# Fused attention and two feed-forward layers: a half tile moved as a half, and two norm rows passed through DRAM

## The chip, the cores and the metric

One core of a Trainium2 chip runs the whole program. The metric is the device time of one execution in microseconds. Matmuls run on TensorE (PE in the rows, its weight loads PEld), elementwise work on VectorE (DVE) and ScalarE (ACT), a few things on GpSimd (POOL); SyncE (SP) issues most transfers, GpSimd the rest.

## What is computed

Four batches of sigmoid attention (12 heads, 448 rows, head size 64) give x of 1792 rows and 768 columns. Then:

```
rms = sqrt(mean(x * x, axis=-1) + 1e-6);  xn = x / rms * rms_g
g = xn @ w_gate;  val = xn @ w_val            # 768 -> 1536
x = (g * sigmoid(g) * val) @ w_out            # 1536 -> 768
h = x @ w_in2                                 # 768 -> 2048
out = (h - tanh(h)) @ w_out2                  # 2048 -> 768
```

All tensors are float32.

## The kernel before

Data lies transposed: channels on the 128 partitions, the 448 rows of a batch along the free axis. A product of two float32 matrices is three matmuls of rounded high parts and low remainders (high by high, high by low, low by high; lines 919 to 923 and 976 to 981), each of 128 x 128 weights on 448 columns.

The two layers work on pairs of batches, (0, 1) and then (2, 3). Two 2 x 2 blocks of weights and of activations are multiplied with seven block products instead of eight (names A11 to S4 on the left, B11 to T4 on the right; lines 819 and 820). Phases Ag and Av are the products with w_gate and w_val, B the one with w_out, C with w_in2, D with w_out2. A job is one pair of weight rows of a phase Ag, Av or C (`seven_units`, 21 groups of three matmuls), or a set of four in B and D (`set_units`; `plain_units`, without the seven-product scheme, for some sets). Jobs for batches (0, 1) come before those for (2, 3) within a layer.

**The left factors.** In its first use, a pair's raw weights are loaded (`load_raw`, 768 KB each), unpacked (`values32`), summed into factors (`sums`, lines 491 to 498) and split into high and low parts (`factors`). `keep` (line 508) also stores the factors in DRAM, in four pieces: (A11, A12), (S1, S2), (S3, S4) and A22. For the pairs that are not in `SPLIT` each piece is a whole tile of 128 x 768 numbers, 384 KB, stored by `put` from SyncE (line 470): 6 pairs of w_gate, 6 of w_val and 6 of w_in2. The tile of the fourth piece holds A21 and A22 as alternating blocks of 128 columns, and only A22 is used later (`one_of`, line 401). In the second use, for batches (2, 3), `two` (line 553) loads each piece with `again` (line 519, 384 KB) and splits it.

**The norm.** In attention `x_end` adds up the squares of x by batch. `norm` (line 671) sums them over the partitions with four one-column matmuls into a bank of PSUM (line 677), scales (line 681, VectorE) and raises to the power -0.5 (line 683, GpSimd): a tile `rc` of 112 x 4 numbers, one for each of the 448 rows. `clear_norm` writes zeros to the bank with one matmul. `spread_norm` (line 691) brings these numbers to all 128 partitions: four VectorE multiplications with an identity matrix (line 698), one float32 matmul with ones (line 702) and a ScalarE copy (line 706). `x_whole` (line 767, its instruction line 770, VectorE) multiplies x with them. For batches 2 and 3 x is put in DRAM (line 669) and reloaded (line 713).

**Order.** All work is entered with `add` into a plan, in program order, with a cost in ns per engine, what it reads and writes, and `after`, the ns until its result is there (`LAND` 4500 and `FAR` 10000 for transfers). `Plan.issue` then simulates the engines: of the work that can start soonest on its engine it takes the one whose deadline is earliest, and writes the instructions out in that order. So every engine runs a fixed order, SyncE too, whose transfers wait in line behind an instruction that waits. A change of a cost or of the program order can change the order on every engine. `mixed` (line 1097) and the list `beside` (line 1129) say beside which units of the main work other work is entered. The norms of batches 2 and 3 are entered beside the last attention batch and behind it (lines 1120 to 1122); their spreads, with `x_units`, from the last job of phase Av of batches (0, 1) to the first job of phase Ag of batches (2, 3) (line 1130). Sums of phases B and D are accumulated in DRAM by GpSimd's transfers with an addition (line 795).

Of the kernel before, what the change touches and what calls it, by code (L numbers as in the profile page):

```python
# [21 lines left out]
P = 128  # L22
# [237 lines left out]
def tile_sigmoid_attention_moe_moe(  # L260
# [38 lines left out]
    def bank(kind="mm"):  # L299
        return slot(kind, ps_p, [P, 512], F32, "ps")  # L300

    def unit(kind, dt=F32):
        return slot(kind, unit_p, [P, S], dt, "unit")
# [85 lines left out]
    def values32(r):  # L389
# [8 lines left out]
            op0=ALU.logical_shift_right, op1=ALU.bitwise_or), [r["t"], z["t"]], [c[0], c[1]])  # L398
        return c

    def one_of(t, x):

        return t.rearrange("p (k e c) -> p e k c", e=2, c=P)[:, x]
# [5 lines left out]
    def factors(j, names, of, reads):  # L409


        n = len(names)
        t = slot("op", wt_p, [P, 2, n, NH], F32R, "wt")
        w = lambda q: t.tile[:, q].rearrange("p n h -> p (n h)")
        hi, lo = (lambda: w(0), lambda: w(1)) if n == 2 else (
            lambda q=q: w(q).rearrange("p (k c) -> p k c", c=P) for q in range(2))
        split(n * NH, hi, lo, of, reads, [t["h"]], [t["l"]])
        use_factors(j, names, t)
        return t
# [62 lines left out]
    def pair_units(ph, i, rs, j):  # L482
        c = []
        d = stored[ph, i] = Slot(None, lambda: dram_p.tile([P, 4, 2, NW], F32, name=f"w{ph}_{i}") if (ph, i) in SPLIT else
                                 dram_p.tile([P, 4, NW], F32, name=f"w{ph}_{i}"))

        def total(to, n, x, y, sub=True):
            add({**dve(NH, psum=False), **pool(NH)}, lambda e: (ENG[e].tensor_sub if sub else ENG[e].tensor_add)(
                one_of(to.tile, n), one_of(x[0].tile, x[1]), one_of(y[0].tile, y[1])), [x[0][x[1]], y[0][y[1]]], [to[n]])

        def sums():
            t = slot("cv", cv_p, [P, NW], F32, "cv")
            a11, a12, a21, a22 = ((x, n) for x in c for n in range(2))
            total(t, 0, a21, a22, sub=False)
            total(t, 1, (t, 0), a11)
            total(c[0], 0, a11, a21)
            total(c[0], 1, a12, (t, 1))
            c.append(t)

        def two(n, names, at):  # L500
            x = c[n]
            keep(None if j is None else factors(j, names, lambda: x.tile, [x[0], x[1]]), at, x)

        def last():
            x = c[1]
            keep(None if j is None else factors(j, ["A22"], lambda: one_of(x.tile, 1), [x[1]]), 3, x)

        def keep(t, at, x):
            if (ph, i) not in SPLIT:
                put(d, at, x)  # L510
                return
            add({"SP": (2200, False)}, lambda e: nc.sync.dma_start(
                out=d.tile[:, at, :, :t.tile.shape[2] * NH], in_=t.tile.bitcast(F32).rearrange("p q n h -> p q (n h)")),
                [t["h"], t["l"]], [d[at]], after=LAND)

        return [lambda: c.append(values32(rs[0])), lambda: c.append(values32(rs[1])), lambda: two(0, ("A11", "A12"), 0),
                sums, lambda: two(2, ("S1", "S2"), 1), lambda: two(0, ("S3", "S4"), 2), last]

    def again(d, at):
        w = slot("again", cv_p, [P, NW], F32, "cv")  # L520
        add({"SP": (1100, False)}, lambda e: nc.sync.dma_start(out=w.tile, in_=d.tile[:, at]), [d[at]], [w[0], w[1]], after=LAND)
        return w
# [18 lines left out]
    def again_units(j):  # L541
        ph, _, i, _ = jobs[j]
        if (ph, i) in SPLIT:
            d = stored[ph, i]

            def load_parts(at, names):
                t = slot("op", wt_p, [P, 2, len(names), NH], F32R, "wt")
                add({"SP": (2200, False)}, lambda e: nc.sync.dma_start(
                    out=t.tile.bitcast(F32).rearrange("p q n h -> p q (n h)"), in_=d.tile[:, at, :, :len(names) * NH]), [d[at]], [t["h"], t["l"]], after=LAND)
                use_factors(j, names, t)  # L550

            return [lambda at=at, names=names: load_parts(at, names) for at, names in enumerate(FACTORS)]
        def two(at, names):
            t = again(stored[ph, i], at)
            of = lambda: t.tile
            if len(names) == 1:
                factors(j, names, lambda: one_of(of(), 1), [t[1]])
            else:
                factors(j, names, of, [t[0], t[1]])

        return [lambda at=at, names=names: two(at, names) for at, names in enumerate(FACTORS)]

# [108 lines left out]
    def norm(b):  # L671
        sq = sqs.pop(b)
        ps = bank("nm")
        ms, rc = (Slot(None, lambda t=t: norm_p.tile([TK, 4], F32, tag=t, name=t)) for t in ("ms", "rc"))
        def sums(e):
            for i in range(4):
                nc.tensor.matmul(  # L677
                    ps.tile[:TK, i:i + 1], lhsT=sq.tile[:, i * TK:(i + 1) * TK], rhs=ones[:, 0:1], start=True, stop=True)

        add({"PE": (1500, False)}, sums, [sq["t"]], [ps["t"]], stream="norm")  # L680
        add(dve(4), lambda e: nc.vector.tensor_scalar(
            out=ms.tile, in0=ps.tile[:TK, :4], scalar1=1.0 / DM, scalar2=EPS, op0=ALU.mult, op1=ALU.add), [ps["t"]], [ms["t"]])
        add({"POOL": (950, True)}, lambda e: nc.gpsimd.tensor_tensor(out=rc.tile, in0=ms.tile, in1=expo, op=ALU.pow),
            [ms["t"]], [rc["t"]])
        rcs[b] = rc, ps

    def clear_norm(b):
        ps = rcs[b][1]
        add({"PE": (250, False)}, lambda e: whole_bank(ps.tile), [], [ps["t"]], stream="norm")

    def spread_norm(b):
        (rc, _), ps2 = rcs.pop(b), bank("nm")
        dg = unit("sq")
        r = rstd[b] = unit("rstd")

        def spread(e):
            for i in range(4):
                nc.vector.tensor_scalar(
                    out=dg.tile[:TK, i * TK:(i + 1) * TK], in0=id_sb, scalar1=rc.tile[:, i:i + 1], scalar2=None, op0=ALU.mult)

        def rows(e):
            nc.tensor.matmul(ps2.tile[:, :S], lhsT=ones[:TK, :], rhs=dg.tile[:TK, :], start=True, stop=True)  # L702

        add({"DVE": (760, True)}, spread, [rc["t"]], [dg["t"]])
        add({"PE": (1500, False)}, rows, [dg["t"]], [ps2["t"]], stream="norm")
        add(act(S, psum=True), lambda e: nc.scalar.copy(r.tile, ps2.tile[:, :S]), [ps2["t"]], [r["t"]])
# [344 lines left out]
    def attn_units(b):  # L1051
        units = []
        for at in range(b * HP, (b + 1) * HP, 2):
            for x in (at, at + 1):
                units.append(lambda x=x: pair_qk(*pairs[x], (0, 1)))
                units.append(lambda x=x: (get_ready(x + 3), pair_qk(*pairs[x], (2, 3))))
            for x in (at, at + 1):
                units.append(lambda x=x: (pair_av(*pairs[x]), pair_end(*pairs[x])))
        return units
# [29 lines left out]
    def by_dve(units):  # L1089
        def run(u):  # L1090
            plan.copies_by = "DVE"
            u()
            plan.copies_by = None

        return [lambda u=u: run(u) for u in units]

    def mixed(units, *others):


        at = [0] * len(others)  # L1100
        for u in units[:2]:
            u()
        units = units[2:]
        for n, u in enumerate(units):
            u()
            for k, o in enumerate(others):
                while at[k] < (n + 1) * len(o) // len(units):
                    plan.later = BESIDE
                    o[at[k]]()
                    plan.later = 0  # L1110
                    at[k] += 1
# [5 lines left out]
    mixed(attn_units(2), [lambda: norm(1), lambda: clear_norm(1), lambda: spread_norm(1), *x_units("A", BATCHES[0], False)], rows_b[at[1]:at[2]])  # L1117
    for j in range(AHEAD):
        load(j)
    mixed(attn_units(3), [lambda: norm(2), lambda: clear_norm(2)], [u for j in range(AHEAD) for u in (*by_dve(conv(j)), lambda j=j: load(j + AHEAD))], rows_b[at[2]:])  # L1120
    norm(3)
    clear_norm(3)
    gates.clear()


# [1 line left out]
    first = {(ph, bs): [j for j in range(len(jobs)) if jobs[j][0] == ph and jobs[j][1] == bs][0] for ph in ("Ag", "C") for bs in BATCHES}  # L1127
    last = {(ph, bs): [j for j in range(len(jobs)) if jobs[j][0] == ph and jobs[j][1] == bs][-1] for ph in ("Av", "C") for bs in BATCHES}
    beside = [
        (last["Av", BATCHES[0]], first["Ag", BATCHES[1]], [lambda: [spread_norm(b) for b in BATCHES[1]], *x_units("A", BATCHES[1], True)], BEHIND),  # L1130
        (last["Av", BATCHES[1]], first["C", BATCHES[0]], x_units("C", BATCHES[0], True), BEHIND),
        (last["C", BATCHES[0]], first["C", BATCHES[1]], x_units("C", BATCHES[1], True), BEHIND),
# [97 lines left out]
```

## Time and profile before

| | us |
|---|---|
| three timed runs, median | 1059.64 |
| lowest and highest of them | 1057.77, 1060.39 |
| the profiled execution | 1060.05 |
| its span, first to last instruction | 1058.2 |
| TensorE busy | 1045.9 |
| VectorE busy | 766.9 |
| ScalarE busy | 689.4 |
| GpSimd busy | 139.7 |

The span is the part of the profiled execution that the trace covers, and all places below are microseconds from its start. Attention takes some 167 us of it, the two layers the rest; the granted clock of TensorE is 1.000 of its full 2.4 GHz throughout. Transfers move 245.64 MB, at a mean of 232 GB/s.

### The profile page before, as it was taken

How to read it: one execution, taken by the hardware profiler on the slowest of the kernel's cores; microseconds unless marked ns; L12 is line 12 of the kernel's file. 1: busy time of each engine (PE TensorE's matmuls, PEld its weight loads, DVE VectorE, ACT ScalarE, POOL GpSimd, SP SyncE). 2: the span in 40 equal slices, each digit the busy share in tenths (PEclk: the TensorE clock that was granted, in tenths of full speed). 3: DMA queues.
4: the chain of work that ended last, by engine and by line, in shares of the span. 5: the costliest groups of instructions: out<-in, count | busy, mean ns of one | idle time of the engine just before them, and what ended most of it. 6: DMA issues, size and time to landing. Idle time of an engine off the chain costs nothing.

```text
span 1058.2 us, 15120 instructions
## 1 busy us (share of the span) xinstructions
PE 1045.9 (99%) x5148; PEld 876.2 (83%) x5148; DVE 766.9 (72%) x1212; ACT 689.4 (65%) x1247; POOL 139.7 (13%) x194
## 2 busy tenths in 40 slices
PE   9999999999999999999999999999999999999998
PEld 3434447999999889999999989999988899999997
DVE  1328976975976895875885777888886888667756
ACT  5766765666675755665665656677675777666652
POOL 1211100000004022111113021000303120003030
PEclk9999999999999999999999999999999999999999
DMA  6888787766759979697879589557959891849393
GB/s 195 275 282 273 239 287 259 280 209 225 255 208 204 343 185 294 205 297 264 290 248 313 166 223 275 209 205 282 199 215 273 241 263 60 281 123 201 113 198 130
DMA packets 105869, 245.64 MB, mean 232 GB/s; under 512 B 27072, under 2 KB 59328, under 8 KB 105792
## 3 DMA queue, kind: packets, MB, share of 16 engines
q1 hardware_dynamic: 82224, 179.63, 50.2%
q0 software_dynamic: 23264, 64.89, 25.0%
q8 instruction: 40, 0.66, 0.3%
q14 instruction: 37, 0.30, 0.1%
q10 hardware_dynamic: 304, 0.16, 0.1%
HBM read 151.44 MB, written 93.19 MB: 231 GB/s over the span
## 4 chain that ended last, share of the span: by engine, by line
PE 88%; issue 5%; DMA 4%; DVE 1%; ACT 1%; POOL 1%; SPq 0%; POOLq 0%; DVEq 0%; ACTq 0%
PE ps L978 43%; PE ps L921 24%; PE ps L612 7%; PE ps L642 7%; PE ps L1003 5%; DMA out<-unit 2%; DMA cv<-wB 1%; DMA wt<-in_w_in 1%; PE ps L331 1%; DVE unit L857 1%; POOL out L795 0%; DVE unit L726 0%; PE ps L702 0%; PE ps L677 0%; ACT wt L324 0%
## 5 line engine op out<-in xcount | busy, mean ns | idle before, releaser
L978 PE MATMUL ps<-unit,wt 128*128 128x448 f32 x2520 | 522.1, 366 | 5.0 <-DVE unit L857 3.6
L978 PEld LDWEIGHTS ps<-unit,wt 128*128 128x128 f32 x2520 | 472.2, 188 | 48.5 <-DVE unit L857 4.7
L921 PE MATMUL ps<-unit,wt 128*128 128x448 f32 x1512 | 313.8, 366 | 0.0
L921 PEld LDWEIGHTS ps<-unit,wt 128*128 128x128 f32 x1512 | 283.8, 188 | 24.3 <-ACT ps L324 0.3
L407 DVE TENSOR_TENSOR wt<-cv,wt 128x768 fp32r<-128x768 f32 (+1 forms) x244 | 215.8, 892 | 76.1 <-ACT wt L324 70.9
L324 ACT CAST wt<-cv 128x768 fp32r<-128x768 f32 (+1 forms) x236 | 185.3, 787 | 108.3 <-PE ps L978 64.0
L324 ACT COPY unit<-ps 128x448 f32<-128x448 f32 x300 | 156.4, 534 | 130.0 <-PE ps L978 49.8
L726 DVE TENSOR_TENSOR unit<-unit 128x448 fp32r<-128x448 f32 x252 | 153.0, 620 | 28.9 <-ACT unit L324 13.4
L324 ACT CAST unit<-unit 128x448 fp32r<-128x448 f32 x252 | 137.9, 567 | 30.8 <-DVE unit L731 9.1
L857 DVE TENSOR_TENSOR unit<-ps,unit 128x448 f32<-128x448 f32 x168 | 103.5, 621 | 47.6 <-PE ps L978 27.6
L731 DVE TENSOR_TENSOR unit<-unit 128x448 f32<-128x448 f32 x144 | 87.4, 619 | 20.1 <-DMA unit<-sumB 10.2
L619 ACT ACTIVATE unit<-ps 128x448 f32<-128x448 f32 (+1 forms) x192 | 84.8, 582 | 6.2 <-PE ps L612 5.9
L612 PE MATMUL ps<-wt 64*128 64x448 f32 (+1 forms) x384 | 77.4, 546 | 0.0
L642 PE MATMUL ps<-unit,cv 128*64 128x448 f32 (+1 forms) x384 | 75.1, 542 | 0.0
L795 POOL DMA_DIRECT2D sumB<-unit x48 | 41.4, 945 | 255.0 <-DVE unit L857 157.2
L396 DVE SCALAR_TENSOR_TENSOR cv<-wt,zero 128x768 uint32<-128x768 uint32 x68 | 64.8, 953 | 11.6 <-ACT zero L324 6.6
L612 PEld LDWEIGHTS ps<-wt 64*128 64x128 f32 (+1 forms) x384 | 32.9, 173 | 39.6 <-issue 29.2
L642 PEld LDWEIGHTS ps<-unit,cv 128*64 128x64 f32 (+1 forms) x384 | 26.3, 136 | 47.5 <-issue 38.0
L1003 PE MATMUL ps<-unit,wt 128*128 128x448 f32 x288 | 60.3, 366 | 1.4 <-ACT unit L324 0.8
L324 ACT CAST zero<-wt 128x768 f16<-128x768 bf16 x52 | 56.1, 1078 | 8.6 <-DVE cv L396 4.6
L1003 PEld LDWEIGHTS ps<-unit,wt 128*128 128x128 f32 x288 | 53.8, 188 | 7.0 <-ACT unit L324 1.6
L665 DVE TENSOR_TENSOR unit<-unit 128x448 f32<-128x448 f32 x20 | 12.5, 623 | 62.3 <-ACT unit L658 62.3
(44 smaller groups left out, 427.1 us busy)
## 6 DMA issues: line engine op xcount, KB each, us to landing
wt<-in_w_out POOLq DMA_DIRECT2D x28, 768.0 KB, 7.4
cv<-wD SPq DMA_DIRECT2D x56, 384.0 KB, 4.9
cv<-wB SPq DMA_DIRECT2D x36, 384.0 KB, 5.4
wt<-in_w_in SPq DMA_DIRECT2D x16, 768.0 KB, 6.8
sumB<-unit POOLq DMA_DIRECT2D x48, 224.0 KB, 6.9
wD<-cv POOLq DMA_DIRECT2D x28, 384.0 KB, 5.6
wt<-in_w_gate SPq DMA_DIRECT2D x12, 768.0 KB, 5.1
wt<-in_w_val SPq DMA_DIRECT2D x12, 768.0 KB, 4.9
```

The costliest lines, as they stand in the source:

```text
L324: add(engines, lambda e: (nc.scalar.copy if e == "ACT" else nc.vector.tensor_copy)(to(), of()), reads, writes)
L396: add(dve(NW, psum=False), lambda e: nc.vector.scalar_tensor_tensor(out=c.tile.bitcast(U32), in0=r.tile[:, :NW, 1], scalar=13, in1=z.tile, ...
L407: add({**dve(n, psum=False), **pool(n)}, lambda e: ENG[e].tensor_sub(lo(), of(), hi().bitcast(F32)), [*reads, *kh], [*kl])
L612: nc.tensor.matmul(ps[i, c].tile[:n, :S], lhsT=t.tile[rows, at:at + n], rhs=t.tile[rows, :S], start=True, stop=True)
L619: add(act(S, psum=True), lambda e: nc.scalar.activation(to.tile[at:at + n, :S], ps.tile[:n, :S], AF.Sigmoid, bias=-math.log(S), scale=1.0 ...
L642: nc.tensor.matmul(ps.tile[i * D:(i + 1) * D, :S], lhsT=v.tile[:n, c, i, :], rhs=a[c][i].tile[:n, :], start=(c == 0), stop=(c == 3))
L726: add({**pool(S), **dve(S, psum=False)}, lambda e: ENG[e].tensor_sub(t["l"].tile, of.tile, t["h"].tile.bitcast(F32)), [of["t"], kh], [kl])
L731: add({**dve(S, psum=False), **pool(S)}, lambda e: ENG[e].tensor_sub(t.tile, x.tile, y.tile), [x["t"], y["t"]], [t["t"]])
L857: add(dve(S), lambda e: nc.vector.tensor_add(t.tile, ps.tile[:, :S], t.tile), [ps["t"], t["t"]], [t["t"]])
L921: nc.tensor.matmul(ps.tile[:, :S], lhsT=part(a), rhs=x[b].tile, start=n in (1, 5) and kp == 0 and q == 0, stop=kp == n_kp - 1 and q == 2, ...
L978: nc.tensor.matmul(ps.tile[:, :S], lhsT=part(a), rhs=x[b].tile, start=n in ((1, 2, 5) if opening else (1, 5)) and i == 0 and q == 0, stop= ...
L1003: nc.tensor.matmul(ps.tile[:, :S], lhsT=wt, rhs=a[p].tile, start=start and i == 0, stop=stop and i == 2, skip_group_check=True)
```

## The change

In the pairs that are not split, the fourth piece is stored and loaded as 128 x 384 numbers, 192 KB: `keep` gathers the A22 blocks out of their tile with the transfer itself, into the first half of the stored row, and `two` loads this half and uses it as it lies. The plan's cost of each of these transfers is 550 instead of 1100.

The norms of batches 2 and 3 are entered beside the first two jobs of phase Ag instead of beside and behind the last attention batch. For these two batches `norm` also stores `rc` as a row of 448 numbers in DRAM from SyncE, and `spread_norm` is one load of that row to all 128 partitions; the VectorE, TensorE and ScalarE instructions of the spread are gone for them.

```diff
--- before.py
+++ after.py
@@ -398,6 +398,9 @@
             op0=ALU.logical_shift_right, op1=ALU.bitwise_or), [r["t"], z["t"]], [c[0], c[1]])
         return c
 
+    def half_of(t):
+        return t[:, :NH].rearrange("p (k c) -> p k c", c=P)
+
     def one_of(t, x):
 
         return t.rearrange("p (k e c) -> p e k c", e=2, c=P)[:, x]
@@ -506,6 +509,10 @@
             keep(None if j is None else factors(j, ["A22"], lambda: one_of(x.tile, 1), [x[1]]), 3, x)
 
         def keep(t, at, x):
+            if (ph, i) not in SPLIT and at == 3:
+                add({"SP": (550, False)}, lambda e: nc.sync.dma_start(
+                    out=half_of(d.tile[:, at]), in_=one_of(x.tile, 1)), [x[1]], [d[at]], after=LAND)
+                return
             if (ph, i) not in SPLIT:
                 put(d, at, x)
                 return
@@ -551,12 +558,13 @@
 
             return [lambda at=at, names=names: load_parts(at, names) for at, names in enumerate(FACTORS)]
         def two(at, names):
+            if len(names) == 1:
+                d, w = stored[ph, i], slot("again", cv_p, [P, NW], F32, "cv")
+                add({"SP": (550, False)}, lambda e: nc.sync.dma_start(out=w.tile[:, :NH], in_=d.tile[:, at, :NH]), [d[at]], [w[0]], after=LAND)
+                factors(j, names, lambda: half_of(w.tile), [w[0]])
+                return
             t = again(stored[ph, i], at)
-            of = lambda: t.tile
-            if len(names) == 1:
-                factors(j, names, lambda: one_of(of(), 1), [t[1]])
-            else:
-                factors(j, names, of, [t[0], t[1]])
+            factors(j, names, lambda: t.tile, [t[0], t[1]])
 
         return [lambda at=at, names=names: two(at, names) for at, names in enumerate(FACTORS)]
 
@@ -682,13 +690,24 @@
             out=ms.tile, in0=ps.tile[:TK, :4], scalar1=1.0 / DM, scalar2=EPS, op0=ALU.mult, op1=ALU.add), [ps["t"]], [ms["t"]])
         add({"POOL": (950, True)}, lambda e: nc.gpsimd.tensor_tensor(out=rc.tile, in0=ms.tile, in1=expo, op=ALU.pow),
             [ms["t"]], [rc["t"]])
-        rcs[b] = rc, ps
+        if b in BATCHES[0]:
+            rcs[b] = rc, ps
+            return
+        d = Slot(None, lambda: dram_p.tile([1, S], F32, name=f"rstd{b}"))
+        rcs[b] = d, ps
+        add({"SP": (650, False)}, lambda e: nc.sync.dma_start(
+            out=d.tile.rearrange("o (i p) -> (o p) i", p=TK), in_=rc.tile), [rc["t"]], [d["t"]], after=15000)
 
     def clear_norm(b):
         ps = rcs[b][1]
         add({"PE": (250, False)}, lambda e: whole_bank(ps.tile), [], [ps["t"]], stream="norm")
 
     def spread_norm(b):
+        if b in BATCHES[1]:
+            d, _ = rcs.pop(b)
+            r = rstd[b] = unit("rstd")
+            add({"SP": (650, False)}, lambda e: nc.sync.dma_start(out=r.tile, in_=d.tile[0].partition_broadcast(P)), [d["t"]], [r["t"]], after=FAR)
+            return
         (rc, _), ps2 = rcs.pop(b), bank("nm")
         dg = unit("sq")
         r = rstd[b] = unit("rstd")
@@ -1117,9 +1136,7 @@
     mixed(attn_units(2), [lambda: norm(1), lambda: clear_norm(1), lambda: spread_norm(1), *x_units("A", BATCHES[0], False)], rows_b[at[1]:at[2]])
     for j in range(AHEAD):
         load(j)
-    mixed(attn_units(3), [lambda: norm(2), lambda: clear_norm(2)], [u for j in range(AHEAD) for u in (*by_dve(conv(j)), lambda j=j: load(j + AHEAD))], rows_b[at[2]:])
-    norm(3)
-    clear_norm(3)
+    mixed(attn_units(3), [u for j in range(AHEAD) for u in (*by_dve(conv(j)), lambda j=j: load(j + AHEAD))], rows_b[at[2]:])
     gates.clear()
 
 
@@ -1127,6 +1144,7 @@
     first = {(ph, bs): [j for j in range(len(jobs)) if jobs[j][0] == ph and jobs[j][1] == bs][0] for ph in ("Ag", "C") for bs in BATCHES}
     last = {(ph, bs): [j for j in range(len(jobs)) if jobs[j][0] == ph and jobs[j][1] == bs][-1] for ph in ("Av", "C") for bs in BATCHES}
     beside = [
+        (first["Ag", BATCHES[0]], first["Ag", BATCHES[0]] + 2, [lambda b=b, f=f: f(b) for b in BATCHES[1] for f in (norm, clear_norm)], BEHIND),
         (last["Av", BATCHES[0]], first["Ag", BATCHES[1]], [lambda: [spread_norm(b) for b in BATCHES[1]], *x_units("A", BATCHES[1], True)], BEHIND),
         (last["Av", BATCHES[1]], first["C", BATCHES[0]], x_units("C", BATCHES[0], True), BEHIND),
         (last["C", BATCHES[0]], first["C", BATCHES[1]], x_units("C", BATCHES[1], True), BEHIND),
```

## Rows read from the trace of the kernel before

**Rows 1.** The page, part 1: busy time, share of the span and instructions.

```profile
PE 1045.9 (99%) x5148; PEld 876.2 (83%) x5148; DVE 766.9 (72%) x1212; ACT 689.4 (65%) x1247; POOL 139.7 (13%) x194
```

**Rows 2.** Waits of PE: waited for, us in total, times, longest us.

```profile
PE ps L978 <- DVE unit L857: 3.6, 3, 2.2
...
PE ps L978 <- ACT unit L324: 1.4, 1, 1.4
PE ps L1003 <- ACT unit L324: 0.8, 2, 0.6
PE ps L1003 <- DVE unit L781: 0.6, 1, 0.6
```

**Rows 3.** Timeline, 340 to 349 us: start, us, engine, line, tiles [idle before, releaser].

```profile
344.10 0.83 ACT L324 CAST wt<-cv 128x768 fp32r<-128x768 f32 x1 [4.59 <-DMA cv<-wB]
...
345.97 0.61 DVE L857 TENSOR_TENSOR unit<-ps,unit 128x448 f32<-128x448 f32 x1
...
346.64 2.69 PE L978 MATMUL ps<-unit,wt 128*128 128x448 f32 x12 [2.16 <-DVE unit L857]
```

**Rows 4.** Chain that ended last, in order of time: start, us, what.

```profile
130.17 0.88 PE ps L677 x8
...
167.63 0.69 PE ps L677 x8
...
329.47 14.55 DMA cv<-wB
...
359.14 0.76 PE ps L702 x2
...
360.51 0.75 PE ps L702 x2
```

**Rows 5.** Timeline of SyncE's queue, 296 to 365 us.

```profile
327.99 0.33 SPq L373 DMA_DIRECT2D wt<-in_w_val  x1
328.41 1.01 SPq L470 DMA_DIRECT2D wAg<-cv  x2
```

**Rows 6.** Transfers, 320 to 346 us: queue (q0 GpSimd's, q1 SyncE's), packets, MB, share.

```profile
q0 software_dynamic: 1789, 3.14, 71.3%
q1 hardware_dynamic: 994, 2.99, 33.3%
```

**Rows 7.** Timeline, 376 to 383 us.

```profile
380.29 0.67 PE L1003 MATMUL ps<-unit,wt 128*128 128x448 f32 x2 [0.18 <-ACT unit L324]
380.88 0.62 DVE L781 TENSOR_TENSOR unit<-unit 128x448 fp32r<-128x448 f32 x1
...
381.55 1.69 PE L1003 MATMUL ps<-unit,wt 128*128 128x448 f32 x7 [0.59 <-DVE unit L781]
```

**Rows 8.** Timeline, 762 to 770 us.

```profile
766.73 1.07 ACT L324 CAST zero<-wt 128x768 f16<-128x768 bf16 x1 [2.43 <-DMA wt<-in_w_in]
...
769.38 0.88 PE L978 MATMUL ps<-unit,wt 128*128 128x448 f32 x3 [0.95 <-DVE unit L857]
```

**Rows 9.** Lines 698 and 683: count, ns minimum/median/maximum, first and last start.

```profile
L698 DVE TENSOR_SCALAR unit<-id_sb,rc x16: 269/272/358, 60.3 to 329.4; 112x112 f32<-112x112 f32 x16
...
L683 POOL TENSOR_TENSOR rc<-ms,expo x4: 1006/1128/1407, 51.8 to 168.7; 112x4 f32<-112x4 f32 x4
```

**Rows 10.** Timeline of SyncE's queue, 140 to 240 us.

```profile
176.12 0.33 SPq L373 DMA_DIRECT2D wt<-in_w_val  x1
```

**Rows 11.** Transfers, 100 to 150 us: packets by size, and queue 1.

```profile
DMA packets 10349, 13.00 MB, mean 260 GB/s; under 512 B 7443, under 2 KB 8344, under 8 KB 10343
...
q1 hardware_dynamic: 9735, 9.79, 60.1%
```

**Rows 12.** Transfers, 150 to 200 us: packets by size, and queue 1.

```profile
DMA packets 5321, 13.68 MB, mean 274 GB/s; under 512 B 1536, under 2 KB 2048, under 8 KB 5318
...
q1 hardware_dynamic: 5318, 13.63, 77.7%
```

## The prediction

> **What bounds the kernel now.** I read the page first: TensorE is busy 1045.9 us of a span of 1058.2 us [rows 1]. Whatever leaves TensorE's stream of matmuls shortens the kernel, and whatever leaves another engine does so only where TensorE waits for it. Second come TensorE's waits: 3.6 us in three waits for the VectorE addition of line 857, 1.4 us in one wait for ScalarE, 0.8 and 0.6 us at line 1003 [rows 2], 6.4 us in all. What is left of the idle time lies before the first matmul and behind the last one; the change touches neither.
>
> Third comes the longest wait, 2.16 us ending at 346.64 us [rows 3]. ScalarE had sat idle 4.59 us for the load of a stored factor of w_out (the cast at 344.10); VectorE stood behind ScalarE, and the addition that TensorE needed came at 345.97, behind both. In the chain of waits that load takes 14.55 us from its issue at 329.47 [rows 4]. Ahead of it in SyncE's queue stand a raw load of w_val (768 KB, at 327.99) and two stores of w_gate factors (384 KB each, from 328.41 on) [rows 5]. The queues say why this is slow: from 320 to 346 us the 12 accumulating transfers on GpSimd's queue hold 71.3% of the 16 engines' time in 1789 packets, SyncE's queue 33.3% in 994 [rows 6] (the shares overlap a little, so they sum to over 100%). So the late load is a matter of transfers ahead and beside, not of an engine.
>
> Fourth, the two other waits near the change. At 381.55 TensorE waits 0.59 us for a VectorE subtraction that starts at 380.88 [rows 7]; with the 0.18 us just before, by the same stage, I count 0.77. At 769.38 it waits 0.95 us behind a ScalarE cast that was idle 2.43 us for a raw load of w_in2 [rows 8], again while accumulating transfers are under way.
>
> **The change part by part.**
>
> *Spreads of batches 2 and 3.* Each one's fp32 matmul appears as two passes: 0.76 us at 359.14 and 0.75 us at 360.51 [rows 4]. TensorE is back to back on both sides, so 1.51 us leave the path. Beside it go eight VectorE multiplications of 272 ns [rows 9], 2.2 us, and two ScalarE copies of a bank, on engines that have room there: counted at nothing. Also gone is the tie of lines 770 and 726 to TensorE's place for the spread; the numbers can be loaded before.
>
> *Norm sums later.* Four one-column matmuls and a clearing matmul per batch move from the last attention batch and its end into the first two jobs of the layers. They cost 0.88 us (batch 2) and 0.69 us (batch 3) in the old places [rows 4]. The new places are in a stream of the same kind as batch 3's, so 0.69 is the price nearest; the gain is 0 to 0.19 us and I take nothing. The squares have long been summed then, so the sums wait for nothing. VectorE waits for them once per batch, GpSimd's power takes 1.13 us [rows 9], and the clearing matmul has ten units of other work in front of it. The bank held over those units is one of eight, and a job takes three.
>
> *Two stores of the row.* Each is 448 single numbers, so 448 packets. SyncE stands at the store until the power is done; behind it wait the stores of w_gate and w_val factors and raw loads like the one at 176.12 [rows 10], which serve jobs two ahead: 42 groups of three matmuls at the plan's 609 ns each, some 25 us. Packets priced: in 100 to 150 us 9735 packets of SyncE's queue, 7443 packets being under 512 B, take 60.1% of 16 x 50 us [rows 11]; in 150 to 200 us 5318, with 1536 small, take 77.7% [rows 12]. Two equations give 16 ns for a small packet (256 B, the length of nearly all of them) and 158 ns for a large one (some 3.5 KB). The two prices bound a store: 448 packets on 16 engines are 0.45 to 4.4 us of transfer time. The reader comes over 100 us later, so I take nothing.
>
> *Two loads of the row, spread to 128 partitions.* 224 KB each, issued somewhere before 359 us. If they fall ahead of the w_out load of 329.47, they cost time: 1920 KB (the raw load, two stores, the load itself) took 14.55 us, 132 KB per us, so 1.7 us each, 3.4 us for both. If they are issued before the accumulations begin, nothing. They have no slot that ties them to the moment, only a row stored long before, and the plan issues what can start; I take nothing and keep 3.4 us for the range.
>
> *Half tiles.* 18 pairs (6 of w_gate, 6 of w_val, 6 of w_in2; two more are stored split and keep their form) store and load 192 KB less each. A stored row turns from one packet of 3072 B into three of 512 B; between the two packet prices by length that is 140 ns against 3 x 27, so 59% remains. A loaded row becomes one of 1536 B, 73 ns, 52%. By itself none of this is on the path; it matters where a late transfer holds TensorE.
> At 346.64: one of four stores of the last w_gate pair is the halved one, and two of the four stand directly ahead of the late load. If it is one of these, 41% of 384 KB, 157 KB, are gone at 132 KB per us: 1.2 us sooner. If it is neither, 0. The ends: all 2.16 us, or the 3.4 us above on the other side. I take -0.5, nearer to 0, since half the chance is for 0.
> At 769.38: the same kind of wait; stores of w_in2 factors share the queue with the raw load. 0 to -0.95, I take -0.3, as one store in four shrinks.
> At 381.55: VectorE does line 726's work for the new batch in this stage; with the spread loaded sooner some of it comes before. 0 to -0.77, I take -0.3.
> The waits at 816 and 823 us (the rest of lines 324 and 857) and at 616 lie where no factor tile is halved or nothing differs: 0.
>
> *How a late load is priced is where the Trainium skill speaks against the change.* My price goes by bytes. In the burst a queue's packets may also take turns: an accumulating packet holds an engine 71.3% x 16 x 26 / 1789 = 0.166 us [rows 6], and 512 packets ahead of and in the late load, 32 per engine, took 14.55 us, 0.45 us a turn, which leaves room for one or two accumulating packets per turn. A store of 384 packets then takes 16 more turns per engine than one of 128, at 0.166 us each 2.7 us more, less the 1.2 us saved at most. "DMA: Bandwidth & Descriptors" of the Trainium skill, section Queues, rings and completion order, has each engine go round between its queue rows packet by packet, a packet being several descriptors. By that rule the term of -0.5 would be up to +2.7 and the sum 1060.6 us; the trace can't tell it from bytes, as its stores there all have equal rows.
>
> *The sum.* -1.51 - 0.5 - 0.3 - 0.3 = -2.6 us against the profiled execution's own 1060.05 us (span 1058.2): 1057.4 us. The three timed runs have their median at 1059.64, 0.41 lower; the forecast then is 0.2% below the median. About 0.3% (3.2 us) is what a measurement of this kernel can tell from no change, so the likeliest outcome is "the same", with the sign of a gain.
>
> **Rivals.**
> A, the forecast: 1057.4, own range 1054.6 (1.51, and the three waits of 2.16, 0.95 and 0.77 gone) to 1060.6 (one halved store by turns). Chance 0.50.
> B, transfers get enough room that all waits behind late transfers go, those at 816 and 823 us (1.4 and 0.5) too: 1060.05 - 1.51 - 2.16 - 0.95 - 1.9 = 1053.5. For it: each of these waits sits behind a transfer in a burst. Against: the last two lie where no factor is halved. Chance 0.18.
> C, the 1.51 us are given back as new waits: the order on every engine is planned anew, and today's 6.4 us of waits are what one such order leaves; another may leave 8. 1060.0. For it: costs in the plan change for 36 transfers. Against: today's order, planned just as freely, leaves only seven waits among 5148 matmuls. Chance 0.14.
> D, slower: packets take turns, and the halved stores in both bursts (before 346 and before 769 us) hold the raw and stored loads back: +2.7 at each, 1060.05 - 1.51 + 5.4 = 1063.9. It decides once a halved store stands ahead of a load that TensorE's additions already wait for, as the one at 329.47 does; with only one such place the time is 1061.2. For it: the 14.55 us. Against: half the bytes, and the store may stand elsewhere. Chance 0.18.
>
> **How the numbers follow.** The time is A's. The range goes from B's 1053.5 to 1062.8, between D's one place and its two; below B and above that some 2 in 10 are left. Faster by over 0.3% (below 1056.5) holds B and about a quarter of A: 0.31. Slower by over 0.3% (above 1062.8) holds most of D and a tail of C: 0.18. Within: 0.51.
>
> **What would show it.** Line 702 must show four passes instead of eight, with 1.5 us less of TensorE. If A holds, the wait near 345 us is under 2.16 us and the load of w_out behind it takes less than 14.55 us; by D it takes more, with the halved store ahead. The loads of the row should land well before the first instruction of line 770 after 331 us. TensorE's waits summed over 6.4 us would mean C or D, and a wait at line 677's new place, or at the clearing matmul, would show that moving the sums was not free. A time below 1053 or above 1064 would need a mechanism that I have not named.

## The result and the profile after

The changed kernel takes 1067.72 us (median of six runs, 1066.19 to 1070.02) against 1059.02 of the kernel before beside it: ratio 1.0088, 95% interval 1.0075 to 1.0101. It is slower by some 9 us, outside the stated range, and on the other side of the forecast. The profiled execution, the slowest of the six, has a span of 1068.2 us, 10.0 more than before.

The page's part 1 of the changed kernel, columns as in [rows 1]:

```profile
PE 1049.6 (98%) x5144; PEld 878.9 (82%) x5144; DVE 765.6 (72%) x1204; ACT 688.3 (64%) x1245; POOL 139.5 (13%) x194
```

Its waits of PE, as in [rows 2]:

```profile
PE ps L997 <- ACT unit L324: 5.7, 2, 4.2
PE ps L997 <- DVE unit L876: 5.3, 2, 3.3
...
PE ps L1022 <- ACT unit L324: 1.1, 2, 0.6
PE ps L1022 <- DVE unit L800: 0.4, 1, 0.4
```

Four matmul instructions are gone, as they should, yet TensorE is busy 3.7 us longer than in [rows 1]. Its waits (lines 997 and 1022 are the old 978 and 1003) are 12.5 us instead of 6.4. The timeline of 160 to 212 us shows where, and what came late:

```profile
167.01 1.07 ACT L324 CAST zero<-wt 128x768 f16<-128x768 bf16 x1 [7.37 <-DMA wt<-in_w_gate]
...
169.08 1.03 DVE L491 TENSOR_TENSOR cv<-cv 128x384 f32<-128x384 f32 x2 [5.44 <-DMA wAv<-cv]
...
172.50 14.64 PE L997 MATMUL ps<-unit,wt 128*128 128x448 f32 x63 [4.22 <-ACT unit L324]
...
187.39 0.33 SPq L373 DMA_DIRECT2D wt<-in_w_gate  x1
...
187.78 0.42 SPq L473 DMA_DIRECT2D wAv<-cv  x1
...
189.21 0.33 SPq L698 DMA_DIRECT2D rstd<-rc  x1
...
201.74 0.56 DVE L491 TENSOR_TENSOR cv<-cv 128x384 f32<-128x384 f32 x1 [4.44 <-DMA wAv<-cv]
...
210.97 1.45 PE L997 MATMUL ps<-unit,wt 128*128 128x448 f32 x3 [1.98 <-DVE unit L876]
```

ScalarE stands 7.37 us for a raw load, VectorE 5.44 and 4.44 us for stores that must have left a tile before it is overwritten, and TensorE 4.22 and 1.98 us behind them. Before, this stretch had no wait of TensorE at all. The row's stores (line 698 of the changed kernel, at 154.15 and 189.21 us) stand just ahead of the late transfers, or among them. The transfers from 188 to 204 us:

```profile
DMA packets 840, 1.73 MB, mean 108 GB/s; under 512 B 496, under 2 KB 496, under 8 KB 838
...
q1 hardware_dynamic: 838, 1.71, 88.2%
...
wAv<-cv SPq DMA_DIRECT2D x3, 384.0 KB, 13.2
wt<-in_w_gate SPq DMA_DIRECT2D x1, 768.0 KB, 13.4
cv<-wB SPq DMA_DIRECT2D x2, 384.0 KB, 13.6
...
rstd<-rc SPq DMA_DIRECT2D x1, 1.8 KB, 12.7
```

The 16 engines are 88.2% taken and move 108 GB/s. A transfer of 1.8 KB takes 12.7 us, and the others of this list 13 to 14 us; so does the store of 187.78, which was issued before it (13.9). The time is not in the row's own packets: in the packet records of this stretch the 496 packets of 4 B (the row's 448 and 48 others) start from 191.4 to 194.3 us and take 9 ns each. The 214 packets of 6144 B, which are those of the raw loads, take 960 ns at the mean and 9.3 us at most; in the whole kernel before, packets of this size take 280 ns at the mean and at most 2.3 us. The store of 187.78 has its last packet started by 193.0 us, yet it lands at 201.7. From 195 to 203 us, when no short packet starts any more, the engines are still taken:

```profile
DMA packets 51, 0.31 MB, mean 39 GB/s; under 512 B 0, under 2 KB 0, under 8 KB 51
...
q1 hardware_dynamic: 51, 0.31, 86.3%
```

That is 86.3% x 16 x 8 us / 51, or 2.2 us for each packet.

After each of the two waits TensorE's granted clock is lower for some microseconds (windows of 10 us; granted clock third from the end):

```profile
170.00:180.00 10.00, 7.50 (x29) 6.80 (x30) 6.10 (x10) 3.55 (x7) 0.00 (x0) 0.83 0.63 226
180.00:190.00 10.00, 10.00 (x55) 9.32 (x54) 6.05 (x11) 8.01 (x12) 1.01 (x1) 1.00 0.61 193
...
210.00:220.00 10.00, 9.03 (x37) 8.21 (x38) 8.67 (x16) 6.38 (x12) 0.00 (x0) 0.83 0.64 227
```

A mean of 0.83 is part of the 10 us at 1.2 GHz, the rest at 2.4. Not every wait of this length is followed by one: after the 2.16 us of [rows 3] the kernel before keeps a granted clock of 1.00. The third such place is near 830 us. In the chain:

```profile
829.94 0.62 DVE unit L876
830.56 0.53 DVE unit L745
831.09 0.55 DVE unit L876
831.64 0.04 issue
831.68 3.25 PE ps L997 x9
```

Nine matmuls take 3.25 us there and 1.8 us elsewhere; the waits of this stretch are 4.8 us, before 1.9.

The account, from the two profiled executions, in us: 150 to 222 us +6.2 of waits and some 3.4 of lower clock (63 matmuls in 14.64 us, against 13.01 in experiment 3, which has no wait there, and 1.8 after the second); near 830 us +2.9 and some 1.6; the waits of [rows 3, 7] together 2.0 less, the one of [rows 8] 0.95 less; the spreads 1.5 less. That is +9.7 of the 10.0 us.

### The profile page after: what moved, and what is told of

Read it like the earlier page. It is cut to its first block, busy times and chain, and to the rows that moved or that the text cites. A ratio compares the mean times of both kernels' runs of the same rounds, so it can differ in the third digit from the quotient of the medians.

```text
span 1068.2 us, 15095 instructions
## 1 busy us (share of the span) xinstructions
PE 1049.6 (98%) x5144; PEld 878.9 (82%) x5144; DVE 765.6 (72%) x1204; ACT 688.3 (64%) x1245; POOL 139.5 (13%) x194
## 4 chain that ended last, share of the span: by engine, by line
PE 68%; issue 9%; DMA 4%; DVE 2%; POOL 2%; ACT 1%; SPq 0%; POOLq 0%; DVEq 0%; ACTq 0%
PE ps L997 40%; PE ps L940 23%; PE ps L1022 5%; DMA wAv<-cv 2%; POOL out L814 2%; DMA out<-unit 1%; DVE wt L410 0%; DVE unit L876 0%; DVE cv L396 0%; ACT unit L324 0%; ACT wt L324 0%; DVE unit L745 0%; DVE cv L491 0%; DVE unit L750 0%; DVE unit L857 0%
## 5 line engine op out<-in xcount | busy, mean ns | idle before, releaser
L750 DVE TENSOR_TENSOR unit<-unit 128x448 f32<-128x448 f32 x144 | 87.3, 619 | 18.3 <-DMA unit<-sumB 8.2
L491 DVE TENSOR_TENSOR cv<-cv 128x384 f32<-128x384 f32 x80 | 43.0, 552 | 15.6 <-DMA wAv<-cv 9.9
```

What stands on the lines that cost most here:

```text
L750: add({**dve(S, psum=False), **pool(S)}, lambda e: ENG[e].tensor_sub(t.tile, x.tile, y.tile), [x["t"], y["t"]], [t["t"]])
```

## The experiments

The store theory: the stores of the row's 448 single numbers hold up all transfers for some 10 us. Its rivals: the half tiles' stores in pieces of 512 B do it; any new order of the plan costs about this much. Each ratio is to the kernel before on the same chip, with its 95% interval.

**1. Half tiles alone.** The kernel before with the new `half_of`, `keep` and `two`; norms and spreads untouched.

```diff
+            if (ph, i) not in SPLIT and at == 3:
+                add({"SP": (550, False)}, lambda e: nc.sync.dma_start(
+                    out=half_of(d.tile[:, at]), in_=one_of(x.tile, 1)), [x[1]], [d[at]], after=LAND)
+                return
...
```


> The kernel before with the half tiles alone; norms and spreads stand as before. Store theory (the 448 single numbers of the row hold the queue's transfers for some 10 us): no wait of TensorE over 1 us between 150 and 220 us, the waits of 2.16 and 0.95 us smaller, 1056 to 1060 us; if the later wait near 830 us belongs to the half tiles' order, up to 1064. Piece theory (the stores in pieces of 512 B are what makes transfers late): waits of 2 us or more between 150 and 220 us again, 1065 us or more. Order theory (any new order leaves about this much): 1062 to 1068 with waits in other places.

Measured: 1059.48 us, ratio 1.0010 (0.9998 to 1.0023). No wait from 150 to 220 us; the one of [rows 3] is gone too. But from 700 to 900 us TensorE has 5.5 us of waits, 4.8 of them in one:

```profile
PE ps L986 <- DVE unit L865: 5.5, 2, 4.8
```

Pieces of 512 B are not what makes transfers late at 170 and 200 us. This version brings no gain either, and a wait near 820 to 830 us comes with it; experiments 5 and 6 tell its bytes from its order.

**2. Norms alone.** The changed kernel with `keep` and `two` of before.

```diff
-            if (ph, i) not in SPLIT and at == 3:
...
-            if len(names) == 1:
-                d, w = stored[ph, i], slot("again", cv_p, [P, NW], F32, "cv")
...
```

> The changed kernel with whole tiles again; late norms and the row through DRAM stay. Store theory: the two waits in 150 to 220 us are there again, 4 and 2 us give or take 2, with the row's second store landing in 10 to 13 us, 1063 to 1068 us. Piece theory: no such waits, 1056 to 1058 us. Order theory: 1062 to 1068 with waits elsewhere.

Measured: 1065.9 us, ratio 1.0075 (1.0060 to 1.0091); TensorE is idle 6.2 us of 150 to 220 us (windows; the second number is TensorE's busy time), and the row's second store lands after 11.9 us:

```profile
150.00:220.00 70.00, 63.83 (x308) 50.30 (x305) 47.71 (x77) 40.10 (x69) 1.48 (x2) 0.98 0.82 236
...
rstd<-rc SPq DMA_DIRECT2D x1, 1.8 KB, 11.9
```

This part alone carries nearly the whole loss.

**3. The row as 112 pieces of 16 B.** The changed kernel, every engine in the same order; the multiplication of line 770 (789 in the changed kernel) takes its operands in the permuted order.

```diff
-            out=d.tile.rearrange("o (i p) -> (o p) i", p=TK), in_=rc.tile), [rc["t"]], [d["t"]], after=15000)
+            out=d.tile.rearrange("o (p i) -> (o p) i", p=TK), in_=rc.tile), [rc["t"]], [d["t"]], after=15000)
...
-            out=x.tile, in0=x.tile, scalar=g_sb[:, c:c + 1], in1=r.tile, op0=ALU.mult, op1=ALU.mult),
+            out=at(x.tile, "i p"), in0=at(x.tile, "i p"), scalar=g_sb[:, c:c + 1], in1=at(r.tile, "p i"), op0=ALU.mult, op1=ALU.mult),
```


> The changed kernel in its own order on every engine; only the row in DRAM is ordered so that each partition's four numbers lie together: 112 pieces of 16 B instead of 448 of 4 B. Store theory: the store lands in 3 to 5 us, the waits of 4.2 and 2.0 us near 172 and 211 us and the lower granted clock behind them are mostly gone, some 8 to 9.6 us less: 1058 to 1060 us, with the wait near 830 us left. Piece and order theories: unchanged, 1066 to 1069 us.

Measured: 1059.84 us, ratio 1.0019 (1.0008 to 1.0030). Seven of the nine microseconds are gone with one access pattern, and as the order is that of the changed kernel, the order is not what cost them. The stores land in 1.8 and 6.2 us, where 3 to 5 was expected, and the stretch is without a wait (windows):

```profile
DMA to landing us min/median/max: 1.8/4.0/6.2
...
150.00:220.00 70.00, 70.00 (x347) 56.48 (x346) 56.00 (x89) 43.74 (x75) 1.01 (x1) 1.00 0.72 237
```

**4. The stores on GpSimd's queue.** The changed kernel in its order, the access pattern unchanged.

```diff
-        add({"SP": (650, False)}, lambda e: nc.sync.dma_start(
+        add({"SP": (650, False)}, lambda e: nc.gpsimd.dma_start(
             out=d.tile.rearrange("o (i p) -> (o p) i", p=TK), in_=rc.tile), [rc["t"]], [d["t"]], after=15000)
```


> The changed kernel in its own order; only the row's two stores go out on GpSimd's queue, with the 448 pieces as they are. If being behind them in SyncE's queue is what counts: 1058 to 1061 us, the transfers of SyncE's queue issued next land in 4 to 8 us. If the engines themselves are held, whatever the queue: 1065 to 1069 us as before this edit, those transfers still landing in 10 us or more.

Measured: 1067.09 us, ratio 1.0082 (1.0064 to 1.0101). Transfers from 189 to 202 us (q0 is GpSimd's queue):

```profile
q1 hardware_dynamic: 334, 1.46, 68.4%
...
q0 software_dynamic: 32, 0.00, 0.3%
...
wt<-in_w_gate SPq DMA_DIRECT2D x1, 768.0 KB, 11.9
wAv<-cv SPq DMA_DIRECT2D x2, 384.0 KB, 10.7
cv<-wB SPq DMA_DIRECT2D x2, 384.0 KB, 10.6
...
rstd<-rc POOLq DMA_DIRECT2D x1, 1.8 KB, 10.8
```

SyncE's transfers are nearly as late (10.6 to 11.9 us, against 13.2 to 13.6) although the row isn't in their queue. The place in line is not what counts; what all queues share is held. This agrees with the Trainium skill, "DMA: Bandwidth & Descriptors", section Issuing engines are not separate DMA queues: transfers from any issuing engine run on the same 16 engines. On this queue the trace records the row as part of 32 packets that take 0.3% of the engines' time, so neither the number of packets nor their own time is the price; the time stands in SyncE's packets.

**5. Half tiles in the old order.** The kernel before, the fourth piece halved, with the plan's costs and dependences of a whole piece, so that every engine keeps its order.

```diff
+                add({"SP": (1100, False)}, lambda e: nc.sync.dma_start(out=half_of(d.tile[:, at]), in_=one_of(x.tile, 1)), [x[0], x[1]], [d[at]], after=LAND)
...
+                add({"SP": (1100, False)}, lambda e: nc.sync.dma_start(out=w.tile[:, :NH], in_=d.tile[:, at, :NH]), [d[at]], [w[0], w[1]], after=LAND)
```


> The kernel before with half tiles whose plan costs and dependences are those of whole tiles, so that every engine keeps the order of before. Bytes theory: the late load of a w_out factor near 346 us lands about 1 us sooner, TensorE's wait there 0.5 to 1.5 us instead of 2.2, ratio to before 0.997 to 0.999. Turns theory (a store in 384 pieces takes more turns from the transfers behind it): that wait 3 to 5 us, ratio 1.002 to 1.005. If the wait of 4.8 us that the half tiles alone showed near 820 us comes from the new order, it isn't here.

Measured: 1057.49 us, ratio 0.9989 (0.9981 to 0.9998), the lowest ratio of all here and the only one below 1 beyond its interval, by little. The load of [rows 4] in this run's chain:

```profile
329.12 12.93 DMA cv<-wB
```

TensorE's waits from 300 to 400 us:

```profile
PE ps L989 <- DVE unit L868: 0.6, 1, 0.6
PE ps L1014 <- DVE unit L792: 0.6, 1, 0.6
PE ps L1014 <- ACT unit L324: 0.2, 1, 0.2
```

12.93 instead of 14.55 us, and a wait of 0.6 instead of 2.16, in one profiled execution of each. The halved store, issued at 323.09 us ahead of the raw load, gives the others room although it goes in 384 pieces; the turns of rival D don't show.

**6. Whole tiles in the new order.** The kernel of experiment 1 with its plan, moving 384 KB again.

```diff
-                    out=half_of(d.tile[:, at]), in_=one_of(x.tile, 1)), [x[1]], [d[at]], after=LAND)
+                    out=d.tile[:, at], in_=x.tile), [x[1]], [d[at]], after=LAND)
...
```


> The kernel with the half tiles alone, in that kernel's order on every engine, but with the transfers moving whole tiles again. Order theory: the wait near 820 us is 4 to 6 us still, and the ratio to before 1.002 to 1.005. Piece theory: it falls under 2 us and the ratio is 0.998 to 1.000.

Measured: 1061.42 us, ratio 1.0026 (1.0014 to 1.0038), with 4.9 us of waits from 780 to 840 us:

```profile
PE ps L986 <- DVE unit L865: 3.5, 1, 3.5
PE ps L986 <- ACT unit L324: 1.4, 1, 1.4
```

The profiled executions of experiments 1 and 6 are the second slowest of theirs, so the ratios weigh more than the size of these waits. With the kernel before and experiments 1 and 5 this is a table of four:

| ratio to before | whole tiles | half tiles |
|---|---|---|
| old order | 1 | 0.9989 |
| order of the halved plan | 1.0026 | 1.0010 |

Halving the fourth piece is worth 0.0011 in the old order. In the new order the difference is 0.0016, but there the two intervals overlap, so that gain is not shown by itself. The order that the plan makes of the lower costs takes 0.0021 to 0.0026 back.

**7. Norms alone, row as 112 pieces.** Experiment 2 with the edit of experiment 3.

```diff
-            out=d.tile.rearrange("o (i p) -> (o p) i", p=TK), in_=rc.tile), [rc["t"]], [d["t"]], after=15000)
+            out=d.tile.rearrange("o (p i) -> (o p) i", p=TK), in_=rc.tile), [rc["t"]], [d["t"]], after=15000)
...
```

> Whole tiles, late norms, and the row through DRAM as 112 pieces of 16 B: the norm part of the change without its single numbers, in the order of the run with the norms only. If the 1.5 us of TensorE that the spreads took come out: no wait over 1 us between 150 and 220 us, ratio to before 0.998 to 0.9995. If a new order gives them back: 1.000 to 1.003, with waits in other places.

Measured: 1059.76 us, ratio 1.0014 (0.9998 to 1.0029). Its waits are 7.1 us in all, one of 1.67 us before 220 us among them. Against experiment 2 the single numbers cost 0.0061 of the time. The interval lies above the 0.998 to 0.9995 that was expected if the 1.5 us of the spreads come out, so no such gain shows; where it goes was not looked for.

**8. The 448 numbers 512 B apart.** The changed kernel in its order; the row is stored spaced, and the spread loads 448 numbers of q instead, so x of batches 2 and 3 is scaled with other numbers.

```diff
-        d = Slot(None, lambda: dram_p.tile([1, S], F32, name=f"rstd{b}"))
+        d = Slot(None, lambda: dram_p.tile([S, P], F32, name=f"rstd{b}"))
...
-            out=d.tile.rearrange("o (i p) -> (o p) i", p=TK), in_=rc.tile), [rc["t"]], [d["t"]], after=15000)
+            out=d.tile.rearrange("(i p) c -> p i c", p=TK)[:, :, 0], in_=rc.tile), [rc["t"]], [d["t"]], after=15000)
...
```


> The changed kernel in its own order; the 448 numbers are stored 512 B apart, so that no two share a line of DRAM (the spread then loads 448 numbers of q in place of the row, same size: x of batches 2 and 3 is scaled with other numbers). Price by piece: the stores land in 10 us or more and the ratio to before stays at 1.006 to 1.009. Price by neighbours in one line: they land in 3 to 6 us, ratio 1.000 to 1.003.

Measured: 1060.0 us, ratio 1.0013 (1.0001 to 1.0026). Line 698, count and ns of an issue, and the us to landing:

```profile
L698 SPq DMA_DIRECT2D rstd<-rc x2: 332/354/376, 154.0 to 184.0; - x2
...
DMA to landing us min/median/max: 2.0/4.0/6.0
```

The transfers from 184 to 194 us, among them the second store:

```profile
DMA packets 1496, 2.80 MB, mean 280 GB/s; under 512 B 542, under 2 KB 899, under 8 KB 1494
...
q1 hardware_dynamic: 1494, 2.77, 85.4%
```

As many single numbers, as many bytes, at the same places of the queue, and 280 GB/s go on beside them; TensorE is busy all 70 us from 150 to 220. So the price is not one per packet: it is paid when the 4 B numbers are neighbours in DRAM. The 16 B pieces of experiment 3 are neighbours too and were as cheap, so with larger and fewer pieces it is not paid.

**9 and 10. Two attempts at a better version.** Experiment 9 is experiment 7 with the half tiles of experiment 5:

```diff
+            if (ph, i) not in SPLIT and at == 3:
+                add({"SP": (1100, False)}, lambda e: nc.sync.dma_start(out=half_of(d.tile[:, at]), in_=one_of(x.tile, 1)), [x[0], x[1]], [d[at]], after=LAND)
+                return
...
```

> Late norms, the row as 112 pieces of 16 B, and half tiles with the plan costs of whole ones, in the order of the run with whole tiles and this row. If half the bytes are worth what they were in the old order (about 0.0011), the ratio to before falls from 1.0014 to 1.000 to 1.0007; a ratio under 0.998 would need the 1.5 us of the spreads to come out here, which that order did not show.

Measured: 1059.06 us, ratio 1.0007 (0.9997 to 1.0017).

Experiment 10 is experiment 5, norms in their old places, with the row as 112 pieces in place of the spreads of batches 2 and 3:

```diff
+        if b in BATCHES[1]:
+            d, _ = rcs.pop(b)
+            r = rstd[b] = unit("rstd")
+            add({"SP": (650, False)}, lambda e: nc.sync.dma_start(out=r.tile, in_=d.tile[0].partition_broadcast(P)), [d["t"]], [r["t"]], after=FAR)
+            return
...
```


> Half tiles with the costs of whole ones, norms in their old places, and for batches 2 and 3 the row through DRAM as 112 pieces of 16 B in place of TensorE's spreads. If TensorE's 1.5 us come out and the order is as good as before's: ratio to before 0.9970 to 0.9985, faster than the half tiles in the old order (0.9989). If the new order takes them: 0.9995 to 1.003, with waits of TensorE over 5 us in all.

Measured: 1057.47 us, ratio 0.9995 (0.9986 to 1.0003). Neither beats experiment 5: in the first the half tiles move the ratio from 1.0014 to 1.0007, within its intervals, and in the second the 1.5 us of TensorE don't come out beyond the interval. Its profiled execution, the slowest of its runs, has 8.0 us of waits, 4.6 of them at one place between 220 and 400 us.

**11. The 448 numbers 64 B apart.** As experiment 8, with another distance.

```diff
-        d = Slot(None, lambda: dram_p.tile([1, S], F32, name=f"rstd{b}"))
+        d = Slot(None, lambda: dram_p.tile([S, 16], F32, name=f"rstd{b}"))
...
```


> As the run with the row's numbers 512 B apart, but 64 B apart (the spread again loads 448 numbers of q). If what costs is that neighbours share a stretch of 64 B or less: the stores land in 3 to 6 us and no wait over 1 us stands between 150 and 220 us. If the stretch is longer: 7 to 13 us, with waits there.

Measured: 1058.94 us (one run). TensorE has one wait of 1.0 us from 150 to 220 us, at the edge of what was expected, and line 698 shows:

```profile
PE ps L997 <- ACT unit L324: 1.0, 1, 1.0
...
DMA to landing us min/median/max: 2.2/4.1/5.9
```

Stores of numbers 64 B apart land as soon as those of numbers 512 B apart. The costly distance of 4 B numbers lies below 64 B; none between 4 and 64 B was tried.

## Why the prediction was wrong

**The step that failed** is "Two stores of the row", in both halves. The price: I took the time of a store's own packets, 0.45 to 4.4 us for 448 of them, as all that it costs. The packet records bear out the small price (9 ns for 4 B, and 18 ns in the kernel before for the 256 B that I had at 16), but the price is not there: the store landed after 12.7 us, and meanwhile the raw loads' packets took 960 ns at the mean, and the transfers beside it 13 to 14 us. The prices came from the attention loads, reads of 256 B from DRAM; these are writes of 4 B, side by side in DRAM, and experiments 8 and 11 show that it is the neighbourhood of single numbers that costs, experiment 3 that pieces of 16 B side by side don't. The cover: I asked only when the row's reader comes, over 100 us later, and set the cost at nothing. The step's own sentence named the stores and raw loads that wait behind SyncE, but only for the time until the power is done, and left out the time in which the store holds up every other transfer. The conversions had no such slack: ScalarE stood 7.37 us for the raw load.

**Spreads.** Right as a removal, 5144 matmul instructions for 5148. That the 1.5 us reach the end is not shown: experiments 7, 9 and 10 have new orders and no gain beyond their intervals.

**Norm sums later.** Free, as forecast: in experiment 3, which has them in the new place, TensorE is busy all 70 us from 150 to 220. (Experiments 7 and 11 each have one wait there, of 1.7 and 1.0 us, whose cause is open.)

**The loads of the row.** They fall at 263 to 266 us, before the accumulations, as taken.

**Half tiles.** The mechanism was right, by bytes; rival D's turns fell with experiment 5. The term of -0.5 at 346 us was too small: the load is 1.6 us sooner and the wait falls by 1.6 in the same order. In that run the halved store stood at 323.09 us, before the raw load and the two stores that I counted, so counting "directly ahead" was the wrong test. The wait at 769 us is gone in the changed kernel and in experiment 5, where I took a third of it. The wait at 381 us hardly changed (0.77 to 0.9).

**The waits at 816 and 823 us**, which I set at no change because no halved tile lies there, grew from 1.9 to 4.8 us in the profiled executions, with a lower clock behind them. That was rival C's mechanism, a new order, and experiments 5 and 6 show it apart from the bytes: the order costs 2.2 to 2.8 us. Which of the moved transfers does it was not tried.

Rival D had the right sign with the wrong mechanism; the cost that decided, 0.0061 to 0.0075 of the time, stood in the text as nothing.

## What to carry to other kernels

Before a small scattered store is called hidden, ask what else is in flight while it runs: a store of neighbouring single numbers holds up everyone's transfers, whatever queue it goes out on, so keep each partition's numbers together, as experiment 3 does. Where a planner orders the work, change bytes and plan costs apart: here the bytes gained about 1 us and the new order lost 2 to 3. The time of a store's own packets is no bound on what it costs: look at how long the packets beside it take.

## What the runs showed of the hardware

A store of 448 neighbouring 4 B numbers into 1.8 KB of DRAM took 8.3 (experiment 2, the first) to 12.7 us (the changed kernel), and held up loads and stores for as long, those of another queue too (experiment 4); with the numbers 64 or 512 B apart it took 2 to 6 us, and as 112 pieces of 16 B 1.8 to 6.2. Its own packets are recorded with 9 ns each; the time shows in other transfers' packets, those of 6144 B with 960 ns at the mean and 9.3 us at most (changed kernel, 188 to 204 us), against 280 ns and 2.3 us in the kernel before.

The Trainium skill, "DMA: Bandwidth & Descriptors", section Specifications, asks for transfers of at least 512 B for full rate and says that below this the engine reads, modifies and writes. Here pieces of 4 B, all below that size, cost 0.0088 of the time side by side and 0.0013 at 512 B apart (experiment 8, the rest of the change included), so size alone doesn't set the price. That the neighbours' writes wait for one another in the memory, and the engines behind them, would fit the packets that are over by 194.3 us and a landing at 201.9, but it was not shown directly.
